# Reordering the end of an attention kernel with top-128 token feed-forward: banks, last rows, last stores, half a projection

## The chip, the cores and the metric

The kernel runs on one core of a Trainium2 chip. The metric is the device time of one execution in microseconds (us). All times below are from one profiled execution and from three timed runs of the kernel before.

## The reference

For 8 batches and 12 heads, attention without softmax: the scores are cut at zero, squared and divided by the sequence length. Its output, 448 rows of 768 columns per batch, is `x`. A gate vector scores the rows; in each batch the 128 rows with the highest scores go through two layers and are added back, weighted by a sigmoid.

```python
scores = scale * np.matmul(q, k.transpose(0, 1, 3, 2))
attn = np.maximum(scores, 0.0) ** 2 / S
return np.matmul(attn, v)
...
scores = np.einsum('bsd,d->bs', x, w_gate)
out = x.copy()
top_idx = np.argpartition(-scores[b], capacity)[:capacity]
xe = x[b, top_idx]
h = np.maximum(xe @ w1, 0.0)
ye = h @ w2
g = 1.0 / (1.0 + np.exp(-scores[b, top_idx]))
out[b, top_idx] = x[b, top_idx] + g[:, None] * ye
```

## The kernel before

The attention is cut into 24 units of four heads: unit `u` belongs to batch `u // 3`. Everything is recorded in one hand-written order, the string `ORDER`: each word is one step, and every engine runs its own instructions in the order in which the words stand. An engine that waits for one of them holds back all that stand behind it on this engine. Between engines only true dependences are waited for.

The steps that matter for the end of the program, with unit or batch as first number:

- `S,u,c,bank` four score products (L247) into two PSUM banks; `R` cuts them at zero into `r_sb` (ScalarE, L275); `Q,u,g` squares a group of them into `a_sb` (VectorE, L260). Group 2 has three of the seven slots, 4 to 6, and groups 0 and 1 have slots 0, 1 and 2, 3.
- `V,u,c,bank` four products of one slot with the values (L268), summed over the seven slots into two banks, `bank` and the next; `X,u,bank,A` writes the sum to `xT_sb` (ScalarE, L275).
- `G,b,i,bank` two products with the gate vector for each unit of the batch (L335); `bc` writes the sums to `bc_sb` (ScalarE); `col` turns them into columns (four small products, L343), `colE` stores those (VectorE, L349).
- `rk,b,j` ranks every row by comparison (VectorE, L359), `hot` makes one-hot columns of the ranks (L439), `xg` gathers the 128 rows by products with them (TensorE, L466), `sel`, `sE` their indices and gates. These are the last batch's way; earlier batches scatter their rows through DRAM (`sc`, `rb`).
- `RT,u,bank` eight transposes of a unit's output into one bank (L295), `RE,u,bank,A` writes them as rows into `x_sb` (ScalarE, L275). `ST,b,cp` stores the rows of one parity of a batch to `out` (L313, through GpSimd's DMA queue).
- `h,b,f,bank` six products of the first layer (L490), eight such blocks; `hE` cuts four of them at zero into `hT` (L275 or L277). `y,b,half,f,bank` two of the eight products of one half of the second layer (L500), `yE` adds the rows with the gate (VectorE, L509), `ADD,b` writes the 128 rows to `out` by index (L514). `xr,7` reads the chosen rows of batch 7 from `out` by index (L478), and so waits until all of batch 7's stores have landed; `yE,7` needs what it reads.

```python
290  ps = banks[:, at, :].bitcast(BF16)
295  product(ps[:, o:o + 128], src.rearrange("r c p -> r (c p)"), ident, o == 0, o == 896,
311  def ST(b, cp, c0=0, c1=HD):
312      rows = out[b].rearrange("(p c) d -> p c d", c=NC)[:, cp:NC:2, c0:c1]
313      nc.gpsimd.dma_start(out=rows,
314                          in_=x_rows[b % NROW][64 * cp:64 * cp + 64, 0:NJ - cp, c0:c1])
498  def y(self, half, f, at):
499      for ff in (f, f + 1):
500          product(banks[:, at, :384], self.hT[:, ff, :],
501                 w2_sb[:, ff, half * 384:half * 384 + 384], ff == 0, ff == NF - 1)
629  for item in ORDER.split():
```

The end of the order (L611 to L620) takes unit 23's values, the gate sums of batch 7, the second layer of batch 5, ranking and gathering for batch 7, both layers of batch 6, and both layers of batch 7.

Of the kernel before, what the change touches and what calls it, by code (L numbers as in the profile page):

```python
# [23 lines left out]
def kernel(  # L24
# [583 lines left out]
    y,4,0,4,5 rb,5 y,4,0,6,5 RT,21,6 xt,5,7 Q,22,2 S,23,1,0 sc,6,0 R,23,0,2,A S,23,5,2 sc,6,3 yE,4,1,4 yE,4,0,5  # L608
    RE,21,6,D V,22,0,4 V,22,1,4 ix,5 xtE,5,7,D V,22,2,4 V,22,3,4 Q,23,1 V,22,4,4 V,22,5,4 R,23,1,0,A sc,6,2
    V,22,6,4 S,23,6,0 h,5,4,7 R,23,5,2,A sc,6,1 h,5,0,6 R,23,6,0,A h,5,1,6 Q,23,0 h,5,2,6 h,5,3,6 X,22,4,A  # L610
    h,5,5,7 V,23,0,4 Q,23,2 V,23,1,4 hE,5,0,6,D V,23,2,4 V,23,3,4 V,23,4,4 V,23,5,4 V,23,6,4 ADD,4 G,7,0,6  # L611
    h,5,6,7 G,7,1,6 ST,6,0 X,23,4,A h,5,7,7 G,7,2,6 bc,7,6,A RT,23,5 ST,6,1 y,5,0,0,4 hE,5,1,7,A col,7,6
    y,5,0,2,4 RT,22,7 RE,22,7,A rb,6 colE,7,6 rk,7,0 y,5,1,0,6 y,5,1,2,6 y,5,1,4,6 y,5,0,4,4 y,5,0,6,4 rk,7,1
    hot,7,1 hot,7,0 y,5,1,6,6 xt,6,7 RE,23,5,A rk,7,3 sig,5 xg,7,0,0 xg,7,1,0 rk,7,2 hot,7,2 hot,7,3 xg,7,2,0
    xg,7,3,0 ix,6 xtE,6,7,A h,6,0,5 ST,5,0 xgE,7,1,0,A yE,5,1,6 yE,5,0,4 h,6,1,5 h,6,2,5 h,6,3,5 h,6,4,2
    xgE,7,0,0,A h,6,5,2 hE,6,0,5,A p,7,0 p,7,1 h,6,6,2 p,7,2 p,7,3 sel,7,7 ST,5,1 ST,7,0 ST,7,1 h,6,7,2 sE,7,0,7
    sE,7,1,-1 sE,7,2,-1 sgl,7 y,6,1,0,0 y,6,1,2,0 ADD,5 xr,7 y,6,0,0,6 y,6,0,2,6 hE,6,1,2,D y,6,1,4,0 y,6,1,6,0
    y,6,0,4,6 sig,6 y,6,0,6,6 h,7,0,4 h,7,4,1 yE,6,1,0 h,7,5,1 h,7,1,4 yE,6,0,6 ADD,6 h,7,2,4 h,7,3,4 h,7,6,1
    h,7,7,1 hE,7,0,4,D hE,7,1,1,A y,7,1,0,2 y,7,0,0,4 y,7,0,2,4 y,7,1,2,2 y,7,0,4,4 y,7,0,6,4 y,7,1,4,2 yE,7,0,4
    y,7,1,6,2 yE,7,1,2 ADD,7  # L620
    """

    ms = {}
# [50 lines left out]
```

## Time and profile before

| what | us |
|---|---|
| timed runs, median (lowest to highest) | 208.15 (207.12 to 208.65) |
| the profiled execution's own time | 208.53 |
| its span, first to last instruction | 206.8 |
| mean granted TensorE clock over the span, share of full speed | 0.986 |

Times in the rows count from the span's start. In a row of the timeline the first number is the start, the second the time from the first start to the last end, `x8` the number of instructions that were merged, and the square bracket says how long the engine sat idle before and what ended that. PE is TensorE, DVE VectorE, ACT ScalarE, POOL GpSimd. The end of a product is modelled, not observed. A POOL row is the time in which GpSimd makes up the DMA, not the transfer.

### The profile page before, as it was taken

The page shows a single profiled execution, that of the slowest core. Times are in us where ns is not written, and L with a number is a line of the kernel's source. Part 1 is how long each engine was busy: PE and PEld are TensorE (multiplying, and loading weights), DVE is VectorE, ACT ScalarE, POOL GpSimd, SP SyncE. Part 2 cuts the span into 40 slices and gives each one's busy share as a digit, 9 for nine tenths or more (in the row PEclk, how much of TensorE's full clock was granted, in tenths as well). Part 3 has the DMA queues.
Part 4 walks back from the last instruction along what each step waited for, and adds up shares of the span by engine and source line. Part 5 has one row for each costly group of instructions (what it writes and reads, how often), then busy time and mean ns, then how long its engine had stood idle before and what let it go on. Part 6 is the DMA issues. An engine that isn't in the chain of part 4 may idle for free.

```text
span 206.8 us, 6982 instructions
## 1 busy us (share of the span) xinstructions
PE 188.7 (91%) x3028; PEld 121.5 (59%) x3028; DVE 173.5 (84%) x274; ACT 166.6 (81%) x216; POOL 106.8 (52%) x131
## 2 busy tenths in 40 slices
PE   7998988998999999998999999999989999899740
PEld 7555644454555657456765665667655857678620
DVE  3679999999999998989899999999878999474320
ACT  2499999999999999998997997999969987473100
POOL 7854991005880079325901788708857198422410
PEclk9999999999999999999999999999999999999995
DMA  6999999994089995998499297999693701999411
GB/s 183 177 204 202 205 204 204 207 214 92 22 123 219 207 214 178 252 214 195 147 277 172 86 203 234 187 213 239 225 227 71 262 13 31 353 296 345 131 58 42
DMA packets 28491, 37.89 MB, mean 183 GB/s; under 512 B 2492, under 2 KB 23334, under 8 KB 28461
## 3 DMA queue, kind: packets, MB, share of 16 engines
q0 software_dynamic: 26864, 35.15, 82.1%
q1 hardware_dynamic: 1308, 1.85, 3.4%
q8 instruction: 23, 0.38, 0.7%
q10 hardware_dynamic: 288, 0.46, 0.6%
q14 instruction: 8, 0.06, 0.1%
HBM read 41.10 MB, written 19.69 MB: 294 GB/s over the span
## 4 chain that ended last, share of the span: by engine, by line
PE 61%; ACT 26%; issue 5%; DVE 3%; DMA 2%; POOLq 1%; ACTq 0%; DVEq 0%
PE banks L215 33%; ACT r_sb L275 23%; PE banks L247 14%; PE banks L268 10%; PE banks L147 2%; ACT xT_sb L275 2%; DMA q_sb<-out_dram,idx 2%; DVE mk L359 1%; PE banks L343 1%; PE banks L154 1%; POOLq L669 1%; DVE a_sb L260 1%; ACT bc_sb L275 0%; DVE hot__3815 L439 0%; DVE orow L509 0%
## 5 line engine op out<-in xcount | busy, mean ns | idle before, releaser
L275 ACT ACTIVATE r_sb<-banks 128x896 bf16<-128x896 f32 x155 | 132.8, 948 | 12.0 <-PE banks L247 9.4
L260 DVE TENSOR_TENSOR a_sb<-r_sb 128x1792 bf16<-128x1792 bf16 (+1 forms) x72 | 87.7, 1241 | 1.0 <-ACT r_sb L275 0.9
L386 POOL DMA_INDIRECT xe_dram<-x_sb,rank_i x28 | 41.4, 1478 | 51.6 <-DVE rank_i L382 37.9
L247 PE MATMUL banks<-qkt 64*64 64x448 bf16 x672 | 58.6, 363 | 5.8 <-ACT r_sb L275 3.7
L268 PE MATMUL banks<-a_sb,v_sb 64*64 64x448 bf16 x672 | 43.6, 351 | 0.8 <-ACT xT_sb L275 0.8
L247 PEld LDWEIGHTS <-qkt 64*64 64x64 bf16 x672 | 22.8, 104 | 28.8 <-issue 17.6
L279 DVE COPY qkt<-banks 128x1792 bf16<-128x1792 bf16 (+1 forms) x25 | 26.2, 1048 | 4.3 <-PE banks L215 3.0
L268 PEld LDWEIGHTS <-v_sb 64*64 64x64 bf16 x672 | 21.5, 106 | 9.9 <-issue 1.8
L215 PE MATMUL banks<-xeT,w_sb 128*128 128x128 bf16 x384 | 25.4, 219 | 0.5 <-DVE xeT L279 0.5
L215 PE MATMUL banks<-w_sb,hT 128*128 128x384 bf16 x128 | 24.6, 327 | 1.4 <-DVE hT L277 1.4
L215 PEld LDWEIGHTS <-w_sb 128*128 128x128 bf16 x384 | 22.0, 98 | 4.2 <-issue 3.4
L275 ACT ACTIVATE xT_sb<-banks 128x896 bf16<-128x896 f32 x19 | 18.0, 947 | 2.4 <-PE banks L268 2.4
L514 POOL DMA_INDIRECT out_dram<-orow,idx x7 | 9.8, 1396 | 19.1 <-DVE orow L509 15.5
L215 PEld LDWEIGHTS <-hT 128*128 128x128 bf16 x128 | 10.9, 98 | 11.1 <-issue 3.6
L277 DVE TENSOR_SCALAR r_sb<-banks 128x896 bf16<-128x896 f32 x13 | 14.1, 1086 | 3.1 <-PE banks L247 2.8
L359 DVE SCALAR_TENSOR_TENSOR mk<-bc_sb,x_sb,tie 128x448 bf16<-128x448 f32 (+4 forms) x32 | 15.2, 500 | 0.2
L215 PE MATMUL banks<-ident,xT_sb 128*128 128x128 bf16 x192 | 14.8, 220 | 0.2 <-ACT xT_sb L275 0.2
L215 PE MATMUL banks<-ident,q_sb 128*64 128x128 bf16 x336 | 14.3, 226 | 0.1
L313 POOL DMA_DIRECT2D out_dram<-x_sb x16 | 10.8, 682 | 7.0 <-ACT g__3828 L405 7.0
L215 PEld LDWEIGHTS <-q_sb 128*64 128x64 bf16 x336 | 10.6, 112 | 5.9 <-issue 5.0
L215 PEld LDWEIGHTS <-xT_sb 128*128 128x128 bf16 x192 | 11.4, 98 | 4.4 <-issue 2.5
L215 PE MATMUL banks<-ident,k_sb 128*64 128x128 bf16 x336 | 13.8, 221 | 0.0
(96 smaller groups left out, 178.3 us busy)
## 6 DMA issues: line engine op xcount, KB each, us to landing
out_dram<-x_sb POOLq DMA_DIRECT2D x8, 768.0 KB
q_sb<-in_q_dram POOLq DMA_DIRECT2D x7, 672.0 KB
k_sb<-in_k_dram POOLq DMA_DIRECT2D x7, 672.0 KB
out_dram<-x_sb POOLq DMA_DIRECT2D x8, 576.0 KB
w_sb<-in_moe_w_dram POOLq DMA_DIRECT2D x2, 1536.0 KB
v_sb<-in_v_dram POOLq DMA_DIRECT2D x7, 336.0 KB
v_sb<-in_v_dram POOLq DMA_DIRECT2D x14, 168.0 KB
xe<-xe_dram SPq DMA_DIRECT2D x7, 193.0 KB, 4.7
```

The source lines that it names most:

```text
L147: nc.tensor.matmul(out=banks[:, 7, 0:128], lhsT=zero[:, 0:128], rhs=zero[:, 0:128], start=True, stop=True, skip_group_check=True)
L215: nc.tensor.matmul(out=out, lhsT=lhsT, rhs=rhs, start=start, stop=stop, skip_group_check=True, **kw)
L247: nc.tensor.matmul(out=banks[col:col + 64, at + x, :S], lhsT=sb[lo:lo + 64, 1, c, hh, :], rhs=sb[lo:lo + 64, 0, :, hh, :], start=True, sto ...
L260: nc.vector.tensor_tensor(out=a, in0=r, in1=r, op=ALU.mult)
L268: nc.tensor.matmul(out=banks[col:col + 64, at + x, :S], lhsT=vs[lo:lo + 64, 2 * i + x, c, :], rhs=a[lo:lo + 64, c - SLOTS[g][0], x, :], st ...
L275: nc.scalar.activation(out=out_, in_=in_, func=func or AF.Copy, scale=scale)
L277: nc.vector.tensor_scalar(out=out_, in0=in_, scalar1=0.0, scalar2=None, op0=ALU.max)
L279: nc.vector.tensor_copy(out=out_, in_=in_)
L313: nc.gpsimd.dma_start(out=rows, in_=x_rows[b % NROW][64 * cp:64 * cp + 64, 0:NJ - cp, c0:c1])
L359: nc.vector.scalar_tensor_tensor(out=dst, in0=self.bc_[:n, t0:S], scalar=self.cols[:n, j:j + 1], in1=tie[:n, j, t0:], op0=ALU.subtract, op ...
L386: done = nc.gpsimd.indirect_dma_start(out=xe_dram[self.b][:, :], out_offset=bass.IndirectOffsetOnAxis(ap=self.rank_i[:, j:j + 1], axis=0), ...
L514: done = nc.gpsimd.indirect_dma_start(out=out[0:self.b + 1].rearrange("b s d -> (b s) d"), out_offset=bass.IndirectOffsetOnAxis(ap=self.id ...
```

## The change

Only words of `ORDER` are changed, all in its last lines. (1) `V,23` and `X,23` use banks 2 and 3 where they used 4 and 5. (2) `RT,22` and `RE,22` stand earlier, behind the first gate products and behind `X,23`; `RT,22` uses bank 5 where it used 7, `RT,23` bank 1 where it used 5; `RE,23` stands right behind `hE,5,1`, and the last six products of batch 5's first layer (`h,5,7`) stand behind `G,7,2`. (3) The two stores of batch 7 become four: columns 0 to 511 and then columns 512 to 767, which is what units 21 and 22, and unit 23, fill. (4) The eight products `y,6,0`, with `yE,6,0` and `ADD,6`, stand behind all of `h,7` and `hE,7`.

```diff
-    h,5,5,7 V,23,0,4 Q,23,2 V,23,1,4 hE,5,0,6,D V,23,2,4 ... V,23,6,4 ADD,4 G,7,0,6
-    h,5,6,7 G,7,1,6 ST,6,0 X,23,4,A h,5,7,7 G,7,2,6 bc,7,6,A RT,23,5 ST,6,1 y,5,0,0,4 hE,5,1,7,A col,7,6
-    y,5,0,2,4 RT,22,7 RE,22,7,A rb,6 colE,7,6 ...
-    hot,7,1 hot,7,0 y,5,1,6,6 xt,6,7 RE,23,5,A rk,7,3 ...
+    h,5,5,7 V,23,0,2 Q,23,2 V,23,1,2 hE,5,0,6,D V,23,2,2 ... V,23,6,2 ADD,4 G,7,0,6
+    RT,22,5 h,5,6,7 G,7,1,6 ST,6,0 X,23,2,A RE,22,5,A G,7,2,6 bc,7,6,A h,5,7,7 RT,23,1 ST,6,1 y,5,0,0,4
+    hE,5,1,7,A RE,23,1,A col,7,6 y,5,0,2,4 rb,6 colE,7,6 ...
...
-    ST,5,1 ST,7,0 ST,7,1 h,6,7,2 sE,7,0,7
-    ... y,6,1,0,0 y,6,1,2,0 ADD,5 xr,7 y,6,0,0,6 y,6,0,2,6 hE,6,1,2,D y,6,1,4,0 y,6,1,6,0
-    y,6,0,4,6 sig,6 y,6,0,6,6 h,7,0,4 h,7,4,1 yE,6,1,0 h,7,5,1 h,7,1,4 yE,6,0,6 ADD,6 h,7,2,4 ...
-    h,7,7,1 hE,7,0,4,D hE,7,1,1,A y,7,1,0,2 y,7,0,0,4 ...
+    ST,5,1 ST,7,0,0,512 ST,7,1,0,512 ST,7,0,512,768 ST,7,1,512,768 h,6,7,2 sE,7,0,7
+    ... y,6,1,0,0 y,6,1,2,0 ADD,5 xr,7 hE,6,1,2,D y,6,1,4,0 y,6,1,6,0 sig,6 h,7,0,4 h,7,4,1 yE,6,1,0 ...
+    h,7,7,1 hE,7,0,4,D hE,7,1,1,A y,6,0,0,6 y,6,0,2,6 y,6,0,4,6 y,6,0,6,6 yE,6,0,6 ADD,6 y,7,1,0,2 ...
```

On ScalarE, behind the two last evictions of values (`xT_sb`, units 22 and 23), one eviction of rows (`x_sb`) moves ahead of the gate sums (`bc_sb`):

```order
 L275 ACTIVATE xT_sb_91<-banks 128x2x448 x2
+L275 ACTIVATE x_sb_93<-banks 128x4x256
 L275 ACTIVATE bc_sb_96<-banks 128x448
 L275 ACTIVATE hT<-banks 128x512
-L275 ACTIVATE x_sb_93<-banks 128x4x256 x2
+L275 ACTIVATE x_sb_93<-banks 128x4x256
 L405 ACTIVATE g__3828<-xe 128x1
```

The rows of unit 22 now come before `bc_sb`; those of unit 23 keep their place behind `hT` of batch 5.

On GpSimd's DMA queue, between the stores of batch 5 (`x_sb_94`) and the row write of batch 5, batch 7's rows (`x_sb_93`) go in four parts:

```order
 L313 DMA out_dram<-x_sb_94 64x4x768
 L313 DMA out_dram<-x_sb_94 64x3x768
-L313 DMA out_dram<-x_sb_93 64x4x768
-L313 DMA out_dram<-x_sb_93 64x3x768
+L313 DMA out_dram<-x_sb_93 64x4x512
+L313 DMA out_dram<-x_sb_93 64x3x512
+L313 DMA out_dram<-x_sb_93 64x4x256
+L313 DMA out_dram<-x_sb_93 64x3x256
 L514 DMA out_dram<-orow,idx 2688x768
```

Two issues more stand ahead of `ADD,5`, and the first two wait for the rows of units 21 and 22 alone.

On VectorE, at the very end, the evictions of `hT` (batch 6, then batch 7), of batch 6's outputs (`orow`) and of batch 7's outputs (`k_sb_86`):

```order
 L277 TENSOR_SCALAR hT<-banks 128x512
-L509 SCALAR_TENSOR_TENSOR orow<-banks,g__3956,xe 128x384 x2
+L509 SCALAR_TENSOR_TENSOR orow<-banks,g__3952,xe 128x384
 L277 TENSOR_SCALAR hT<-banks 128x512
-L509 SCALAR_TENSOR_TENSOR k_sb_86<-banks,g__3932,q_sb_83 128x384 x2
+L509 SCALAR_TENSOR_TENSOR orow<-banks,g__3952,xe 128x384
+L509 SCALAR_TENSOR_TENSOR k_sb_86<-banks,g__3934,q_sb_83 128x384 x2
```

The second half of batch 6's outputs now follows batch 7's first `hT`, as its products follow `h,7` on TensorE.

## Rows read from the trace of the kernel before

**Rows 1.** The chain that ended last, from 170 us: start, us, what
```profile
176.44 0.82 ACT xT_sb L275
...
192.46 3.91 DMA q_sb<-out_dram,idx
```

**Rows 2.** The timeline from 170 us: the last scores, squares and stores
```profile
174.04 0.36 PE L247 MATMUL banks<-qkt 64*64 64x448 bf16 x4
...
175.52 0.92 ACT L275 ACTIVATE r_sb<-banks 128x896 bf16<-128x896 f32 x1 [1.05 <-PE banks L247]
...
176.47 1.56 DVE L260 TENSOR_TENSOR a_sb<-r_sb 128x2688 bf16<-128x2688 bf16 x1 [0.89 <-ACT r_sb L275]
```

**Rows 3.** The timeline of TensorE from 178.26 us: the last twelve value products
```profile
178.09 0.76 PE L268 MATMUL banks<-a_sb,v_sb 64*64 64x448 bf16 x12
```

**Rows 4.** The timeline from 170 us: gate sums, transposes and rows
```profile
178.89 0.92 ACT L275 ACTIVATE xT_sb<-banks 128x896 bf16<-128x896 f32 x1 [1.64 <-PE banks L268]
...
180.22 0.54 PE L215 MATMUL banks<-xT_sb,wg_col 128*128 128x448 bf16 x2
...
180.59 0.61 PE L215 MATMUL banks<-ident,xT_sb 128*128 128x128 bf16 x8
180.79 0.54 ACT L275 ACTIVATE bc_sb<-banks 128x448 f32<-128x448 f32 x1 [0.98 <-PE banks L215]
...
181.04 0.49 PE L215 MATMUL banks<-w_sb,hT 128*128 128x384 bf16 x2
...
181.46 0.40 PE L343 MATMUL banks<-unit_f,bc_sb 1*128 1x1 f32 x4
...
182.78 1.94 ACT L275 ACTIVATE x_sb<-banks 128x1024 bf16<-128x1024 bf16 x2 [0.95 <-PE banks L215]
```

**Rows 5.** The timeline from 170 us: the layers of batches 6 and 7
```profile
186.47 2.51 PE L215 MATMUL banks<-xeT,w_sb 128*128 128x128 bf16 x42
...
188.07 0.60 ACT L275 ACTIVATE hT<-banks 128x512 bf16<-128x512 f32 x1 [0.53 <-PE banks L215]
...
189.26 2.76 PE L215 MATMUL banks<-w_sb,hT 128*128 128x384 bf16 x16
...
189.58 0.68 DVE L277 TENSOR_SCALAR hT<-banks 128x512 bf16<-128x512 f32 x1
...
191.86 2.84 PE L215 MATMUL banks<-xeT,w_sb 128*128 128x128 bf16 x48
...
195.31 0.69 DVE L277 TENSOR_SCALAR hT<-banks 128x512 bf16<-128x512 f32 x1 [2.63 <-PE banks L215]
195.49 0.60 ACT L275 ACTIVATE hT<-banks 128x512 bf16<-128x512 f32 x1 [5.50 <-PE banks L215]
...
196.05 2.77 PE L215 MATMUL banks<-w_sb,hT 128*128 128x384 bf16 x16 [1.35 <-DVE hT L277]
198.21 1.27 DVE L509 SCALAR_TENSOR_TENSOR k_sb<-banks,g__3932,q_sb 128x384 f32<-128x384 f32 x2 [2.22 <-PE banks L215]
```

**Rows 6.** The timeline from 170 us: what GpSimd issues
```profile
173.85 1.58 POOL L514 DMA_INDIRECT out_dram<-orow,idx  x1 [0.30 <-issue]
...
175.46 2.60 POOL L313 DMA_DIRECT2D out_dram<-x_sb  x4
...
185.01 1.27 POOL L313 DMA_DIRECT2D out_dram<-x_sb  x2 [6.95 <-ACT g__3828 L405]
...
187.35 1.04 POOL L514 DMA_INDIRECT out_dram<-orow,idx  x1 [1.07 <-DVE rem L430]
...
192.46 1.04 POOL L478 DMA_INDIRECT q_sb<-out_dram,idx  x1 [3.98 <-DVE orow L509]
...
193.81 0.99 POOL L514 DMA_INDIRECT out_dram<-orow,idx  x1 [0.24 <-issue]
...
199.76 0.97 POOL L514 DMA_INDIRECT out_dram<-k_sb,idx  x1 [4.88 <-DVE k_sb L509]
```

**Rows 7.** A window while four stores are under way: busy per engine, clock, DMA, GB/s
```profile
178.00:184.00 6.00, 6.00 (x71) 3.96 (x63) 2.56 (x9) 3.17 (x5) 0.06 (x1) 1.00 1.29 407
```

More of the change, by code (lines that the diff above doesn't have):

```diff
@@ L610 @@
     V,22,6,4 S,23,6,0 h,5,4,7 R,23,5,2,A sc,6,1 h,5,0,6 R,23,6,0,A h,5,1,6 Q,23,0 h,5,2,6 h,5,3,6 X,22,4,A
-    h,5,5,7 V,23,0,4 Q,23,2 V,23,1,4 hE,5,0,6,D V,23,2,4 V,23,3,4 V,23,4,4 V,23,5,4 V,23,6,4 ADD,4 G,7,0,6
-    h,5,6,7 G,7,1,6 ST,6,0 X,23,4,A h,5,7,7 G,7,2,6 bc,7,6,A RT,23,5 ST,6,1 y,5,0,0,4 hE,5,1,7,A col,7,6
[L613 to L620, printed above, removed]
+    h,5,5,7 V,23,0,2 Q,23,2 V,23,1,2 hE,5,0,6,D V,23,2,2 V,23,3,2 V,23,4,2 V,23,5,2 V,23,6,2 ADD,4 G,7,0,6
+    RT,22,5 h,5,6,7 G,7,1,6 ST,6,0 X,23,2,A RE,22,5,A G,7,2,6 bc,7,6,A h,5,7,7 RT,23,1 ST,6,1 y,5,0,0,4
+    hE,5,1,7,A RE,23,1,A col,7,6 y,5,0,2,4 rb,6 colE,7,6 rk,7,0 y,5,1,0,6 y,5,1,2,6 y,5,1,4,6 y,5,0,4,4
+    y,5,0,6,4 rk,7,1 hot,7,1 hot,7,0 y,5,1,6,6 xt,6,7 rk,7,3 sig,5 xg,7,0,0 xg,7,1,0 rk,7,2 hot,7,2 hot,7,3
+    xg,7,2,0 xg,7,3,0 ix,6 xtE,6,7,A h,6,0,5 ST,5,0 xgE,7,1,0,A yE,5,1,6 yE,5,0,4 h,6,1,5 h,6,2,5 h,6,3,5
+    h,6,4,2 xgE,7,0,0,A h,6,5,2 hE,6,0,5,A p,7,0 p,7,1 h,6,6,2 p,7,2 p,7,3 sel,7,7 ST,5,1 ST,7,0,0,512
+    ST,7,1,0,512 ST,7,0,512,768 ST,7,1,512,768 h,6,7,2 sE,7,0,7 sE,7,1,-1 sE,7,2,-1 sgl,7 y,6,1,0,0 y,6,1,2,0
+    ADD,5 xr,7 hE,6,1,2,D y,6,1,4,0 y,6,1,6,0 sig,6 h,7,0,4 h,7,4,1 yE,6,1,0 h,7,5,1 h,7,1,4 h,7,2,4 h,7,3,4
+    h,7,6,1 h,7,7,1 hE,7,0,4,D hE,7,1,1,A y,6,0,0,6 y,6,0,2,6 y,6,0,4,6 y,6,0,6,6 yE,6,0,6 ADD,6 y,7,1,0,2
+    y,7,0,0,4 y,7,0,2,4 y,7,1,2,2 y,7,0,4,4 y,7,0,6,4 y,7,1,4,2 yE,7,0,4 y,7,1,6,2 yE,7,1,2 ADD,7
     """
```

## The prediction

> **What bounds the kernel now.** I read the chain of waits first, then the timeline of the last 35 us engine by engine, then what GpSimd issues, since every edit lies there. Three stretches set the end.
>
> First, unit 23's values. The chain says that they wait for the eviction of unit 22's values [rows 1]. The timeline shows a second wait that ends with it: the square of slots 4 to 6 runs 176.47 + 1.56 = 178.03 [rows 2], and the last twelve value products, which need it, start at 178.09 [rows 3]. Two waits are tied there, and the chain names one.
>
> Second, from the gate sums to the gathered rows. The two last gate products start at 180.22, `bc_sb` is ready at 180.79 + 0.54 = 181.33, and the four column products start at 181.46 [rows 4]. Behind them VectorE works without a gap through `rk` and `hot`, and TensorE waits for it before the last gathers. So a delay of the column products moves all that follows.
>
> Third, from `h,6` on TensorE runs in one piece: `h,6` from 186.47, `y,6` from 189.26, `h,7` from 191.86, and then it sits idle for the two `hT` evictions until `y,7` starts at 196.05 [rows 5]. `ADD,7` follows at 199.76 [rows 6]. The read-back `xr,7` lands at 192.46 + 3.91 = 196.37 [rows 1], 1.84 before the first `yE,7` at 198.21 [rows 5]: it isn't the bound, although the chain runs over it.
>
> One thing is odd in that gap. The 48 products of `h,7` end at 191.86 + 2.84 = 194.70, and the two evictions start 0.6 and 0.8 behind that [rows 5], though the first needs only products that stand earlier. The last scores end at 174.04 + 0.36 = 174.40 and their eviction starts at 175.52, 1.1 later [rows 2]. Both times GpSimd is making up an indexed row write, from 193.81 and from 173.85 [rows 6]. It isn't always so: a row write also ran from 187.35, and `hT` of batch 6 started at 188.07 [rows 5, 6], 0.1 behind its 24th product (186.47 + 23 × 0.056 + 0.22 = 187.98).
>
> **The change part by part.** Pitches, start to start: a 128-column product 0.056 (eight transposes, 180.59 to 181.04), a gate product 0.185 (180.22 to 180.59) [rows 4], a product of `y` 2.60/16 = 0.1625 (189.26 to 191.86) [rows 5].
>
> (1) Other banks. Without the wait for unit 22's eviction, slots 0 to 3 can run earlier; slots 4 to 6 still need the square that ends at 178.03, and they started 0.06 behind it. Banks 2 and 3 were last read by an eviction that stands ahead of the one at 175.52 [rows 2], so no new wait comes in. Between 0 and 0.06 gained, taken as 0.
>
> (2) Rows at once. On TensorE eight transposes (0.45) come in ahead of the last gate products and six products of `h,5,7` (0.34) go out behind them: these start 0.11 later, at 180.33. Behind them now stand two gate products, six, eight transposes and two of `y`: 180.33 + 0.37 + 0.34 + 0.45 + 0.33 = 181.82 for the column products, against 181.46. `bc_sb` would be ready at 181.44, so TensorE sets it: **0.36 lost**. On ScalarE the rows of unit 22 (1.94/2 = 0.97) run from the end of `X,23`, 178.89 + 0.92 = 179.81, to 180.78, and `bc_sb` is due at 180.90. That cover is 0.1 wide; without it the row eviction would cost up to 0.97. I take 0. That unit 23's rows come earlier gives nothing: the first gathers have time, as TensorE waits for `hot`.
>
> (3) Stores in two parts. GpSimd issues four instead of two, about 0.64 each (1.27/2 [rows 6]). The first two need unit 22's rows, so they are made up from about 181 instead of 185.01 and queue behind the four stores issued from 175.46; the second two follow unit 23's rows at about 183. GpSimd was idle for 6.95 ahead of 185.01, and `ADD,5` has to wait for its outputs till past 187, so the issues are hidden. `xr,7` no longer waits for late stores but for its indices, near 190, and lands near 194. As its landing had slack, **0**. The slack pays only if something else shrinks by more than 1.84.
>
> (4) Half a projection behind `h,7`. Everything from `h,6` comes 0.36 late: `y,6` at 189.62, the second `hT` of batch 6 from 189.94 to 190.63. Before, eight products of `y,6` stood ahead of those that need it; now four: 189.62 + 0.65 = 190.27. TensorE waits until 190.68 (0.05 from eviction to product, as 196.00 to 196.05): **0.41 lost**. Four more end at 191.33, and `h,7` starts there, 0.53 earlier than before. Its 48 products take 2.67, so `y,6,0` runs 194.00 to 195.30. Batch 7's first `hT`, if released at once, is done near 194.2 and the second near 194.8, so `y,7` starts at 195.30 against 196.05. If the release is as late as before, the first `hT` is done near 195.47, and `y,7` starts at 195.52: 0.2 dearer. I take the prompt one, since no row write stands there any more.
>
> Idle time before was 196.05 − 194.53 = **1.52 gained**. The sum is −1.52 + 0.36 + 0.41 = −0.75; `y,7`, its evictions and `ADD,7` keep their spacing: `ADD,7` at 199.01. `ADD,6` moves behind `yE,6,0` (195.5 to 196.1) and is made up from 196.4 to 197.4, clear of `ADD,7`. The execution of 208.53 becomes 207.78. The median of the timed runs lies 0.38 below that execution, within their spread of 1.5; I forecast **207.8**, between the two ways of counting.
>
> A rule against the way I read the gap: the Trainium skill, Perfetto Trace Analysis, section Tensor Engine Instruction, says the end shown for a product is an estimate, so the engine may really finish later. Here that fits: the evictions of batch 7 start 0.6 and 0.8 behind the shown end. By it the sum is the second rival.
>
> **The rivals.** (a) *The late release moves with the row write.* `ADD,6` is now made up at 196.4 to 197.4, and the first `yE,7` is due at 198.21 − 0.75 = 197.46. If that release comes 1.1 late, as that of the scores did, the two evictions run from 198.56 to 199.83 and `ADD,7` goes out at 200.1: 0.35 later than before, 208.9, **slower**. It decides from a delay of 0.75 on. For it: two late cases with a row write; against it: the case at 187.35 was prompt, and those two stood in or ahead of streams of 128-column products. (b) *The products themselves ended 0.6 late.* Then that time is TensorE's, `y,6,0` follows 0.6 later, and `y,7` starts at 195.9: 208.4, no change. Against it: `hT` of batch 6 was prompt in the same kind of stream. (c) *All releases prompt.* The 1.1 at 174.40 goes as well, in runs where it doesn't occur: 206.7. But where the kernel before has a prompt `hT` of batch 7 too, its `y,7` starts near 194.8 and the time is near 207.3; then the change, with its two losses, is 0.5 slower than that. (d) *The stores land one after another.* Two stores took from 185.01 to 192.46 until the read-back could start, 3.7 each [rows 6]. Four in a row from 181 would take 14.9, so `xr,7` would start near 196.2, land at 200.1, and hold the first `yE,7` 2.65 longer: 210.4, **slower**. Against it: during the four earlier stores 407 GB/s flowed for 6 us [rows 7], so queued stores overlap. The Trainium skill, DMA: Bandwidth & Descriptors, section on the anatomy of one DMA, gives 2.0 us plus bytes over 436 GB/s for each; four one after another would be 11.2 us by that estimate, and it speaks for the same rival; the rate in that window disagrees with a fixed cost that adds up.
>
> **How the numbers follow.** The forecast (207.3 to 208.2) has 0.45, (a) 0.18, (b) 0.15, (c) 0.17, (d) 0.05. Leaving out (d) and the outer part of (c) and (a), the range is 206.6 to 209.0. More than 1% (2.1 us), about what a measurement can tell from no change, needs 206.1 or 210.2: faster 0.05, within 1% 0.90, slower 0.05.
>
> **What would show it.** In the changed trace the last value products should still start near 178.1; column products near 181.8; a new idle gap of 0.4 before the fifth product of `y,6`; `h,7` near 191.3; no gap between `h,7`, `y,6,0` and `y,7`; `xr,7` made up near 190; `ADD,7` near 199.0. The forecast is wrong if the column products come at 181.5 or earlier, if `y,7` waits for `hT`, or if `yE,7` waits for `xr,7` or starts more than 0.3 behind its products.

## The result, and the profile after

The changed kernel takes 204.65 us (median of 5 runs, 204.33 to 205.28) against 207.56 of the kernel before (median of 5 runs beside it, 207.03 to 208.65): ratio 0.9842, 95% interval 0.981 to 0.9874. It is 1.6% faster; the forecast was no change, 207.8, and 204.65 lies below the range. The profiled execution took 204.92, its span is 203.2, and its mean granted clock 0.999. The two profiled executions lie 3.6 apart, the two medians only 2.9: the profiled execution of the kernel before, 208.53, was a slow one for that kernel. The clock is no cause: in the kernel before, 39 of the 40 slices of the page show 9 tenths, and only the last one, behind `ADD,7`, shows 5.

The timeline of the changed kernel, stretch by stretch as [rows 2] and [rows 4 to 6] show it for the kernel before:

```profile
174.42 2.58 POOL L514 DMA_INDIRECT out_dram<-orow,idx  x1 [0.30 <-issue]
...
174.61 0.36 PE L247 MATMUL banks<-qkt 64*64 64x448 bf16 x4
...
175.41 0.92 ACT L275 ACTIVATE r_sb<-banks 128x896 bf16<-128x896 f32 x1 [0.36 <-PE banks L247]
...
176.35 1.56 DVE L260 TENSOR_TENSOR a_sb<-r_sb 128x2688 bf16<-128x2688 bf16 x1 [0.20 <-ACT r_sb L275]
...
179.70 1.02 ACT L275 ACTIVATE x_sb<-banks 128x1024 bf16<-128x1024 bf16 x1
...
180.79 0.54 ACT L275 ACTIVATE bc_sb<-banks 128x448 f32<-128x448 f32 x1
...
181.01 1.27 POOL L313 DMA_DIRECT2D out_dram<-x_sb  x2 [1.39 <-ACT x_sb L275]
...
181.79 0.40 PE L343 MATMUL banks<-unit_f,bc_sb 1*128 1x1 f32 x4
...
183.03 1.27 POOL L313 DMA_DIRECT2D out_dram<-x_sb  x2 [0.75 <-ACT g__3828 L405]
...
190.65 0.82 PE L215 MATMUL banks<-w_sb,hT 128*128 128x384 bf16 x4 [0.25 <-DVE hT L277]
...
191.17 1.04 POOL L478 DMA_INDIRECT q_sb<-out_dram,idx  x1 [2.36 <-DVE hT L277]
191.31 2.84 PE L215 MATMUL banks<-xeT,w_sb 128*128 128x128 bf16 x48
...
193.52 0.69 DVE L277 TENSOR_SCALAR hT<-banks 128x512 bf16<-128x512 f32 x1 [1.32 <-PE banks L215]
...
193.99 4.06 PE L215 MATMUL banks<-w_sb,hT 128*128 128x384 bf16 x24
...
197.29 0.99 POOL L514 DMA_INDIRECT out_dram<-orow,idx  x1 [5.02 <-issue]
197.44 1.27 DVE L509 SCALAR_TENSOR_TENSOR k_sb<-banks,g__3934,q_sb 128x384 f32<-128x384 f32 x2 [1.33 <-PE banks L215]
198.99 0.97 POOL L514 DMA_INDIRECT out_dram<-k_sb,idx  x1 [0.63 <-DVE k_sb L509]
```

And the timeline of TensorE from 178 us, which answers to [rows 3]:

```profile
177.97 0.76 PE L268 MATMUL banks<-a_sb,v_sb 64*64 64x448 bf16 x12
```

Up to `ADD,7` TensorE's and VectorE's positions came within 0.05 of the forecast: column products at 181.79 (181.82), the new gap before the fifth product of `y,6` until 190.65 (190.68), `h,7` at 191.31 (191.33), `y,6,0` and `y,7` as one block of 24 without a gap, the first `yE,7` at 197.44 (197.46), `ADD,7` at 198.99 (199.01). Two positions on GpSimd were off and cost nothing: `xr,7` is made up at 191.17 instead of near 190, and `ADD,6` at 197.29 instead of 196.4. So `ADD,7` goes out 0.77 earlier than in [rows 6], and the span is 3.6 shorter. The other 2.8 lie behind `ADD,7`: 206.8 − 199.76 = 7.0 before, 203.2 − 198.99 = 4.2 after. No engine shows work there. The waits of SP's queue (SyncE) from 195 to 210 us do show the difference (columns: us in total, times, longest). The kernel before:

```profile
SPq L669 <- DMA out_dram<-k_sb,idx: 27.3, 1, 27.3
SPq L669 <- PEq L669: 3.3, 2, 2.8
```

The changed kernel:

```profile
SPq L669 <- DMA out_dram<-orow,idx: 24.2, 1, 24.2
SPq L669 <- DMA out_dram<-k_sb,idx: 1.4, 1, 1.4
SPq L669 <- PEq L669: 0.9, 2, 0.5
```

Here SP waits at the end of the program, line 669 being behind the kernel's last step. First it waits for the last indexed writes, then for the other engines to finish; that second wait falls from 3.3 to 0.9. TensorE's queue stands in the row as the releaser, but releasers are inferred from semaphores, and TensorE has had nothing to do since `y,7`. The instruction that is late is on GpSimd: its last drain, an instruction at line 669 whose record stands in the trace but in none of the rows. It starts 0.23 or 0.24 ahead of `ADD,7` and lasts 6.51 in the kernel before and 3.68 in the changed one, which is the whole difference; behind its end 0.79 is left in both. It isn't the transfer: `ADD,7` lands 3.02 behind its start in both, and in all twenty profiles of this case the last packet of GpSimd's queue ends 2.7 behind that start, while the end of the span follows the drain's end by 0.8 to 1.0. The Trainium skill, Perfetto Trace Analysis, section DMA Instruction — SWDGE (GPSIMD), says that the row of a DMA on GpSimd ends when the descriptors are made, not when the data has moved. The trace agrees: the row of `ADD,7` is 0.97 long in both, and its transfer lands 3.02 behind its start.

### The profile page after: what moved, and what is told of

The parts are those of the page before. It is cut to its first block, busy times and chain, and to the rows that moved or that the text cites. A ratio compares the mean times of both kernels' runs of the same rounds, so it can differ in the third digit from the quotient of the medians.

```text
span 203.2 us, 6985 instructions
## 1 busy us (share of the span) xinstructions
PE 188.6 (93%) x3028; PEld 120.9 (59%) x3028; DVE 173.2 (85%) x274; ACT 166.6 (82%) x216; POOL 108.9 (54%) x133
## 3 DMA queue, kind: packets, MB, share of 16 engines
q0 software_dynamic: 27344, 35.15, 84.1%
## 4 chain that ended last, share of the span: by engine, by line
PE 60%; ACT 25%; issue 6%; DVE 4%; DMA 2%; POOL 1%; POOLq 1%; ACTq 0%; DVEq 0%
PE banks L215 34%; ACT r_sb L275 23%; PE banks L247 14%; PE banks L268 11%; DMA kf<-in_k_dram 2%; ACT xT_sb L275 2%; DVE mk L359 1%; PE banks L343 1%; POOLq L669 1%; DVE qkt L279 1%; DVE a_sb L260 1%; PE banks L154 1%; POOL q_sb L478 1%; POOL out_dram L514 0%; ACT bc_sb L275 0%
## 5 line engine op out<-in xcount | busy, mean ns | idle before, releaser
L514 POOL DMA_INDIRECT out_dram<-orow,idx x7 | 10.8, 1540 | 27.0 <-DVE orow L509 16.3
L313 POOL DMA_DIRECT2D out_dram<-x_sb x18 | 12.1, 679 | 2.1 <-ACT x_sb L275 1.4
```

Of the source, the lines that this page charges most:

```text
L313: nc.gpsimd.dma_start(out=rows, in_=x_rows[b % NROW][64 * cp:64 * cp + 64, 0:NJ - cp, c0:c1])
L514: done = nc.gpsimd.indirect_dma_start(out=out[0:self.b + 1].rearrange("b s d -> (b s) d"), out_offset=bass.IndirectOffsetOnAxis(ap=self.id ...
```

## The experiments

Read is, in each profile, the **end**: from the start of `ADD,7` to the end of the span. All edits are to the kernel before.

**Which edit?** Two theories: N, that the row write moved next to `ADD,7` (edit 4) shortens the end; C, that the two stores more on GpSimd's queue (edit 3) do. All four kernels were timed on one chip, where the kernel before took 207.25; the brackets are 95% intervals of the ratio to it.

Edit 4 alone:

```diff
-    ... xr,7 y,6,0,0,6 y,6,0,2,6 hE,6,1,2,D ... yE,6,0,6 ADD,6 h,7,2,4 ... hE,7,1,1,A y,7,1,0,2
+    ... xr,7 hE,6,1,2,D ... h,7,2,4 ... hE,7,1,1,A y,6,0,0,6 ... yE,6,0,6 ADD,6 y,7,1,0,2
```

> Edit 4 alone (half a projection behind the last first layer; banks, rows and stores as before). In the changed kernel the time from the issue of ADD,7 to the span's end is 4.2 us, before it was 7.0. Theory N (neighbour: the program's last wait on GpSimd is short when another indexed write was made up just ahead of ADD,7): ADD,7 near 198.6, 4.2 behind it, time near 204.5. Theory C (count: it is the two more stores on GpSimd's queue): the end stays 7.0 long, time near 207.4.

Measured (10 runs): 207.02, ratio 1.0001 [0.9968, 1.0034]; end 206.6 − 199.53 = 7.1.

Edit 3 alone:

```diff
-    ST,7,0 ST,7,1
+    ST,7,0,0,512 ST,7,1,0,512 ST,7,0,512,768 ST,7,1,512,768
```

> Edit 3 alone (batch 7's stores in four parts, rows evicted as late as before). Theory N: nothing at the end changes, 7.0 from ADD,7 to the end, time within 0.5 of before. Theory C: ADD,7 as before near 199.8, then 4.2 to the end, time near 205.3.

Measured (4 runs): 203.74, ratio 0.9857 [0.9797, 0.9916]; end 202.3 − 198.03 = 4.3.

Edits 1 and 2 (banks and early rows, stores and half projection as before):

```diff
-    V,23,0,4 ... X,23,4,A ... RT,23,5 ... RT,22,7 RE,22,7,A ... RE,23,5,A
+    V,23,0,2 ... RT,22,5 ... X,23,2,A RE,22,5,A ... RT,23,1 ... RE,23,1,A
```

> Edits 1 and 2 alone (other banks, rows earlier; two stores, y,6,0 ahead of h,7). Both theories: no change of the 7.0 at the end. By the forecast's terms the column products come 0.36 later and nothing gives it back, unless the release of batch 7's first hT is prompt now: ADD,7 near 200.1 with a late release, near 198.9 with a prompt one. Time 208.5 or 207.3.

Measured (10 runs): 207.36, ratio 1.0006 [0.9978, 1.0033]; end 205.9 − 198.84 = 7.1.

Edits 1, 2 and 3, without 4:

> The changed kernel without edit 4. Theory N: 7.0 from ADD,7 to the end, time near 207 to 208.5. Theory C: 4.2, time near 204.5 to 205.7.

Measured (4 runs): 204.01, ratio 0.9854 [0.9797, 0.991]; end 202.7 − 198.46 = 4.2.

N falls, C holds: each kernel with edit 3 has the short end and the whole gain, each without it has the long end and no gain. In these four the end takes one of two lengths and nothing between.

**What about the stores?** One execution each, on two chips where the kernel before took 204.31 and 203.25 us, so the end is compared, not the time. The list of DMA queues counts the packets of GpSimd's queue, the pieces in which its data goes out (columns: packets, MB, share). Kernel before, then `one_split`, then `rows_two`:

```profile
q0 software_dynamic: 26864, 35.15, 82.1%
```

```profile
q0 software_dynamic: 27136, 35.15, 85.5%
```

```profile
q0 software_dynamic: 26896, 35.15, 84.2%
```

A store by columns adds a packet for each row that is cut (64 × 4 = 256) and 16 more, 272 in all; a store cut between rows adds 16. Divided by 16 engines, that is 17 and 1 for each. The megabytes don't change.

```diff
 one_split
-    ST,7,0 ST,7,1
+    ST,7,0,0,512 ST,7,0,512,768 ST,7,1
 early_two
-    ST,0,0 ... ST,0,1
+    ST,0,0,0,512 ST,0,0,512,768 ... ST,0,1,0,512 ST,0,1,512,768
 rows_two (two arguments more in ST: the first and last row of each partition)
-    ST,7,0 ST,7,1
+    ST,7,0,0,768,0,2 ST,7,1,0,768,0,2 ST,7,0,0,768,2,4 ST,7,1,0,768,2,4
 early_eight (the same for ST,0,1, ST,1,0 and ST,1,1)
-    ST,0,0
+    ST,0,0,0,256 ST,0,0,256,512 ST,0,0,512,768
```

> The kernel before with only the first of batch 7's two stores split into columns 0 to 511 and 512 to 767: 104 DMAs on GpSimd's queue instead of 103 (105 in the changed kernel and in stores_only). Read is the time from the start of ADD,7's make-up to the span's end: 7.0 in the kernel before, 4.2 with both stores split. If the size of the last stores' pieces is what matters (big pieces are still under way or still being cleared up behind ADD,7), one big store is left and the end stays near 7.0 or shortens by about half, to 5.6. If the number of DMAs decides, by a step, it is 7.0 or 4.2 and nothing between; which, is not known beforehand.

> The kernel before with its end untouched, but the two stores of batch 0, some 130 us earlier, split into columns 0 to 511 and 512 to 767: 105 DMAs on GpSimd's queue, as in the changed kernel, and as many pieces. If only the number of DMAs over the whole program counts, the end (ADD,7 to the span's end) is 4.2 and the time near 204, as with batch 7's stores split. If it counts where the stores stand, the end is 7.0 and the time 207.3.

> The kernel before with batch 7's two stores split by rows instead of columns: each piece is still one row of 768 columns, so the number of pieces is that of the kernel before, and the number of DMAs is 105. If the number of DMAs decides, the end is 4.2 and the time near 204; if the number of pieces or their size decides, the end stays 7.0 and the time 207.3.

> The kernel before with the four stores of batches 0 and 1 split into three each, 256 columns wide: 111 DMAs on GpSimd's queue, eight more than before, so that the last one uses the same of the eight semaphores in turn as in the kernel before. If the semaphore or the remainder of the count by eight decides, the end is 7.0 as before; if a number of DMAs over some bound decides (104 or 105 and more), it is 4.2. If only the place counts, it is 7.0 too, which early_two tells apart.

The rows of `ADD,7` in `early_two` (span 199.0) and `rows_two` (span 201.4):

```profile
194.73 0.97 POOL L514 DMA_INDIRECT out_dram<-k_sb,idx  x1 [2.47 <-DVE k_sb L509]
```

```profile
194.17 0.96 POOL L514 DMA_INDIRECT out_dram<-k_sb,idx  x1 [3.70 <-DVE k_sb L509]
```

Then `plus9` (stores of batch 0 cut by rows, one row by columns), `plus64`, `plus128` and `plus256` (stores of batches 0 to 3 cut into two to four by columns), as in:

```diff
 plus64
-    ST,0,0 ... ST,0,1 ... ST,1,0
+    ST,0,0,0,512 ST,0,0,512,768 ... ST,0,1,0,512 ST,0,1,512,768 ... ST,1,0,0,256 ST,1,0,256,512 ST,1,0,512,768
```

> The kernel before with its end untouched and the two stores of batch 0 cut up by rows and a little by columns, so that GpSimd's queue carries 144 packets more than before (27008 instead of 26864, nine for each of the 16 engines). 0 and 2 more for each engine gave a long end (ADD,7's start to the span's end 7.0 and 7.2), 17, 30 and 120 more a short one (4.2 to 4.5). This run lies between and tells where the step is: a long end if a window of some ten packets is unlucky, a short one if it is narrower.

> The kernel before with its end untouched and 1024 packets more on GpSimd's queue in early stores (64 for each engine). If any number above a bound gives the short end, ADD,7 to the span's end is 4.2 to 4.5. If the packets are counted round a circle of 64 places for each engine, or of 32, the end is long again, 7.0. If neither the number of packets nor a circle decides but the size of some pieces, 4.2 to 4.5.

> The kernel before with its end untouched and 2048 packets more on GpSimd's queue in early stores (128 for each engine). Long end, 7.0, if the packets are counted round a circle of 128 places for each engine (or of 32 or 64); short, 4.2 to 4.5, if a bound decides or another circle.

> The kernel before with its end untouched and 4096 packets more on GpSimd's queue in early stores (256 for each engine). Long end, 7.0, if the packets are counted round a circle of 256 places for each engine (or of 32, 64 or 128); short, 4.2 to 4.5, if a bound decides or another circle.

What was measured, with the three kernels of the next question:

| kernel | DMAs more | packets more, for each engine | end, us |
|---|---|---|---|
| before | 0 | 0 | 206.8 − 199.76 = 7.0 |
| rows_two | 2 | 2 | 201.4 − 194.17 = 7.2 |
| plus9 | 5 | 9 | 201.5 − 194.40 = 7.1 |
| one_split | 1 | 17 | 199.3 − 194.84 = 4.5 |
| stores_only | 2 | 30 | 202.3 − 198.03 = 4.3 |
| early_two | 2 | 30 | 199.0 − 194.73 = 4.3 |
| plus64 | 4 | 64 | 198.8 − 194.38 = 4.4 |
| early_eight | 8 | 120 | 199.1 − 194.64 = 4.5 |
| plus128 | 8 | 128 | 199.3 − 194.72 = 4.6 |
| plus256 | 16 | 256 | 201.2 − 196.17 = 5.0 |
| plus600 | 40 | 600 | 205.7 − 199.84 = 5.9 |
| plus900 | 60 | 900 | 218.4 − 211.28 = 7.1 |
| plus1200 | 80 | 1200 | 225.2 − 220.37 = 4.8 |

`early_two` settles the place: stores cut some 120 us before the end (they are made up at about 80) shorten it as much as those of the last batch. `rows_two` settles the unit: with as many DMAs as `early_two` but pieces as large as before, the end stays long. The remainder by eight falls as well (`early_eight` is short), and so do circles of 32, 64, 128 and 256 packets for each engine, by which the end would be long again at a multiple (`plus64`, `plus128` and `plus256` are short). What decides, as far as these runs go, is the number of packets on GpSimd's queue over the whole program: the end falls by 2.6 between 9 and 17 more for each engine, and from 30 more on it rises slowly. One thing is not separated: nearly all packets added are pieces of cut rows, so the runs don't tell whether the 16 that come with each DMA count as well.

**A bound or a saw-tooth?** Either a bound was passed once, or the end rises with the packets and falls again and again, like the teeth of a saw.

```diff
 plus600 (all ten stores of batches 0 to 4; plus900: seven each; plus1200: eight each, and the two of batch 5 in six each)
-    ST,0,0
+    ST,0,0,0,160 ST,0,0,160,320 ST,0,0,320,480 ST,0,0,480,640 ST,0,0,640,768
```

> The kernel before with the ten stores of batches 0 to 4 cut into five each by columns: 9600 packets more on GpSimd's queue, 600 for each of the 16 engines. Read is GpSimd's end, from ADD,7's make-up to the span's end. Among the short ends it rose from 4.2 (30 packets more for each engine) over 4.6 (128 more) to 5.0 (256 more), some 0.0035 us for each packet more. Theory of a saw-tooth: the wait at the end grows with the packets that have gone out since a last clearing-up, and falls by 2.8 us whenever one more clearing-up fits in, as between 9 and 17 packets more; by it the end is here 4.2 + 570 x 0.0035 = 6.2. Theory of a bound: above it the end is short for good, about 4.2 to 5.0 here.

> The kernel before with the ten stores of batches 0 to 4 cut into seven each by columns: 14400 packets more on GpSimd's queue, 900 for each of the 16 engines. By the saw-tooth a tooth is about 2.8 / 0.0035 = 800 packets for each engine long, so the next fall comes near 810 more and the end is here about 4.2 + 90 x 0.0035 = 4.5, shorter than with 600 more. By a bound it is no shorter than with 600 more: 4.2 to 5.0 if that one was short, and if the rise simply goes on, 7.2.

> The kernel before with the ten stores of batches 0 to 4 cut into eight each and the two of batch 5 into six each, by columns: 19200 packets more on GpSimd's queue, 1200 for each of the 16 engines. From 30 to 900 packets more for each engine the end (ADD,7's make-up to the span's end) rose from 4.2 to 7.1, and the one known fall, by some 2.7 us, lies between 9 and 17 more, from an end of 7.1. If it falls each time it comes to some 7.1 (saw-tooth with a tooth of about 900 packets for each engine), the next fall came a little above 900 more and the end is here 4.2 + 290 x 0.0033 = 5.2, under 6. If the fall was a single event and the rise goes on, it is 4.2 + 1170 x 0.0033 = 8.1.

`plus600` measured 5.9, beside the 6.2 of the saw-tooth. `plus900` missed: I had put the next fall at 810 more, and the end was 7.1, so the tooth is longer than that guess. `plus1200` showed the fall, 4.8 where a rise that goes on gave 8.1. So it is the shape of a saw-tooth, of which two falls and the rise between them were seen, each point in one execution: a rise of some 2.9 over nearly 900 packets for each engine, a fall from 7.1, and again; the second fall lies between 900 and 1200. `plus1200` also cuts stores of batch 5, which `plus900` doesn't; that the place is without effect was shown with 30 packets more alone. The times of these three kernels are longer (207.52, 220.43, 226.99); why was not followed up, and only their ends are read.

**Is the rest of the change worth anything?** All three were timed on one chip, six runs each, where the kernel before took 203.29 (202.59 to 204.34).

> The changed kernel itself, beside the two others of this call. It was 0.984 of the kernel before. If its gain is the short end alone, it stands within 0.5% of edit 3 alone and of the early split, on either side.

> Edit 3 alone again, on the same chip as the changed kernel. From the traces its ADD,7 went out at 198.03 against 198.99, since the late column products (0.4) and the gap in y,6 (0.4) of edits 2 and 4 are not paid and hT of batch 7 was prompt in it; so 0.5 to 1.0 us (0.2 to 0.5%) faster than the changed kernel. If edits 1, 2 and 4 are worth what was forecast for edit 4, it is 0.7 slower instead.

> The kernel before with only batch 0's stores split, 130 us before the end. By the theory that the number of packets over the whole program decides, ratio to the kernel before 0.984 to 0.988, the same as edit 3 alone within 0.3%. If part of edit 3's gain came from the earlier stores of batch 7, it is slower than edit 3 alone by that part.

| kernel | us (lowest to highest) | ratio to before, 95% interval | column products, `ADD,7`, us between |
|---|---|---|---|
| changed kernel | 201.36 (200.69 to 201.96) | 0.9899 [0.9867, 0.9931] | 178.15, 195.35, 17.20 |
| edit 3 alone | 200.55 (200.15 to 201.46) | 0.9863 [0.9832, 0.9895] | 177.70, 194.77, 17.07 |
| batch 0's stores split | 200.39 (199.74 to 200.62) | 0.9846 [0.9817, 0.9874] | 177.47, 194.54, 17.07 |

The early split is the fastest of the three, and all its runs are below all runs of the changed kernel. It changes nothing at the end of the order at all. Edit 3 alone is 0.8 below the changed kernel in its median, but their runs overlap. So edits 1, 2 and 4 together brought nothing. Whether they cost 0.8 to 1.0, as these medians say, is not settled: edit 4 alone and edits 1 and 2 alone were 1.0001 and 1.0006 of the kernel before.

## Why the prediction was wrong, point by point

**The step that failed** is the last one of the sum: "`y,7`, its evictions and `ADD,7` keep their spacing", and from `ADD,7` at 199.01 straight to an execution of 207.78. That held the 7.0 behind `ADD,7` constant. It was 4.2 there, and these 2.8 are the whole error: 207.78 − 2.83 = 204.95, and the execution took 204.92. With it fails the price of part (3): the stores were costed at 0 by their place on the queue and their landing, and nothing was asked about what they leave behind at the end of the program. All signs that I named as proof of an error lay ahead of `ADD,7`, so none of them appeared and the forecast was wrong all the same. A second term was wrong without showing in the sum: the 1.52 credited to edit 4, see (4).

**(1) Other banks: right.** The square ends at 176.35 + 1.56 = 177.91 and the last twelve value products start 0.06 behind it, as in [rows 2, 3].

**(2) Rows at once: right in mechanism, a little dear.** From the last twelve value products to the column products it is 181.79 − 177.97 = 3.82, against 181.46 − 178.09 = 3.37 [rows 3, 4]: 0.45, forecast 0.36. The cover on ScalarE held, narrowly: the rows of unit 22 end at 179.70 + 1.02 = 180.72, and `bc_sb` starts at 180.79 (forecast 180.78 and 180.90).

**(3) Stores: made up as forecast, price wrong.** They are made up at 181.01 and 183.03 (forecast 181 and 183). Rival (d) falls: by the semaphore updates in the trace the four land at 187.83, 189.09, 189.74 and 190.22, not 3.7 apart, and the first `yE,7` waits for its products. (In its sum 181 + 14.9 is 195.9, not 196.2.) That `xr,7` would wait for its indices alone was wrong too: it is made up 0.95 behind the last of these landings, as it was 0.93 behind the last landing, 191.53, in the kernel before. It lands at 195.25, with 2.2 to spare. The price of the edit was −2.8, as above.

**(4) Half a projection: the positions right, the gain not a gain.** Idle time and gap came as forecast: column products to `ADD,7` took 18.30 in [rows 4, 6] and 17.20 in the changed kernel, 1.10 less, where 1.52 − 0.41 = 1.11 was worked out. But that stretch is 17.20 in all three profiles with edit 4, and 17.06 or 17.07 in ten others, whose layers stand in the order of before (`stores_only`, `no_half`, `edit3_again` and `early_two_again` among them); in `banks_rows`, `early_two` and `one_split` it is 17.28, 17.39 and 17.97, and in the three kernels with 600 packets more and up 18.16 to 22.21. Most of the 1.52 us of idle time that I gave edit 4 credit for was a late release of `hT` in the one execution that I had read: `y,7` starts 196.05 − 191.86 = 4.19 behind `h,7` there and 194.33 − 191.37 = 2.96 in `stores_only`. That leaves 0.29 of the 1.52, less than the 0.41 that edit 4 loses, and against a prompt execution it costs 17.20 − 17.07 = 0.13. Rival (c) had said so, for the case that "the kernel before has a prompt `hT` of batch 7 too", and had 0.17. The timed runs agree: edit 4 alone was 1.0001 of before.

**Rivals (a) and (b)** fall: with `ADD,6` made up at 197.29 the first `yE,7` came at 197.44, not 1.1 late; and `hT` of batch 7 started at 193.52, behind products that had started at 191.31, as promptly as that of batch 6. The late release of the scores also went: the eviction waits 0.36 there instead of 1.05 [rows 2], although GpSimd makes up the row write during it, 174.42 to 177.00. So a neighbouring row write alone doesn't make a release late, against what I read out of [rows 6]. That the column products still came where I had put them has some luck in it: the scores start 0.57 later than before (174.61 against 174.04), and the prompt release makes up for it.

The span adds up as 0.33 (column products later) − 1.10 (from there to `ADD,7`) − 2.83 (end) = −3.60.

**What stays open:** which work of GpSimd its long drain is. The saw-tooth would fit a clearing-up of what has gone through its queue, done now and then and once at the end, so that the last one is long or short by how much has gathered; that is argued, and no run here shows the clearing-up itself. The Trainium skill, DMA: Bandwidth & Descriptors, section SWDGE vs HWDGE vs iDMA, says that GpSimd appends a descriptor pair for each operation to rings in SBUF. No run here shows these rings, or whether a tooth of some 900 to 1200 packets has to do with them. Open too is why a release is late in some executions.

## What to carry to other kernels

Cost the end behind the last instruction as a term of its own: subtract the last step's start from the span, and ask which edit could change it, even one far away. Where a program issues DMAs from GpSimd, cutting two early stores in two can be worth 2.8 us, and taking such a cut back can cost them, by the number of packets; so try it as a cheap experiment, and whoever compares two orders that differ in their stores should compare their ends first, or the whole gain is put down to the wrong edit. An idle gap of one profiled execution is no cost of the kernel until a second execution shows it: here two of them, 1.1 us at the last scores and 1.2 at `hT` of batch 7, weren't there again in most of the other profiles: the first came back in `half_only` alone, the second in none.

## What the runs showed of the hardware

The time from the last DMA on GpSimd's queue to the end of the program ran through a saw-tooth of 4.2 to 7.2 us with the number of packets on that queue: long at 26864, 26896 and 27008 packets, short from 27136 on, 5.0 at 30960, 5.9 at 36464, 7.1 at 41264, and 4.8 at 46064. With 27344 packets it didn't depend on where in the program the added ones were, and two more DMAs without cut rows (26896) left it long; the megabytes are the same, 35.15 or 35.16 in all. With the same number of packets it repeats within 0.1 us: 7.0 to 7.1 in three profiles of 26864, 4.2 to 4.3 in seven of 27344, on several chips. It ends with GpSimd's last drain, 6.51 and 3.68 us long at these two numbers, while the last transfer lands 3.02 behind its start at both. A row of SP's waits helps to spot it: the wait on `PEq` sums to 3.3 to 3.8 us where the end is 7.0 to 7.2, and to 0.7 to 0.9 where it is 4.2 to 4.6.
